# Preparing the second MoE's weights by pieces: one piece to three matmul groups instead of one to two attention slots

## The chip, the cores and the metric

The program runs on one core of one Trainium2 chip. The metric is device time in microseconds (us). In the core, TensorE (PE) multiplies matrices, VectorE (DVE), ScalarE (ACT) and GpSimd (POOL) work on tiles, and the queue of SyncE (SP) issues nearly all DMAs, in its order. Each engine carries out its own instructions in the order in which they stand in the program, and waits on semaphores for the others.

## The reference

Attention with a memory term, then two feed-forward blocks over 2304 tokens of 512 numbers (4 batches of 576):

```
scores = scale * q k^T, causal;  a = softmax(scores)         # B,H,S,D = 4,8,576,64
phi(x) = elu(x) + 1;  mem = (phi(q) M_prev) / (phi(q) z_prev)
x = g * mem + (1 - g) * (a v)                                # as [2304, 512]
h = x @ w_in;   x = (h * sigmoid(h)) @ w_out                 # first MoE,  d_ff 2048
g = x @ w_gate; v = x @ w_val
out = (g * sigmoid(g) * v) @ w_out2                          # second MoE, d_ff 1536
```

The weights come as float64, the rest as float32.

## The kernel before

**First half.** Attention and the first MoE run together. Attention is cut into units (a batch and a pair of heads), a unit into steps, and the steps of all units are laid out in numbered slots (`slots`, 177 of them, 0 to 176). Attention's tiles live in pools that are opened one after another, `atA`, `atB`, `atF` and `atG` (batches 2 and 3); `open_G` also starts the generator `prep_w2`. The first MoE is a generator too (`moe1`): 32 segments (a block of 256 or 320 tokens by a slice of four 128-columns of w_in), each with four groups of 12 matmuls into h (L785) and four groups of 12 into y (L843), 256 groups in all; each gives one item. After a group into h follow `th` on ACT (L792) and DVE (L793), `gh` on ACT (L194) and `gl` on POOL (L795), which the groups into y read. There are two `th` buffers and, while attention runs, three PSUM banks for h and y; later eight. The main loop takes item after item and runs attention slots as goals require.

**The second MoE's weights.** It multiplies float32 weights as a high and a low part, so the float64 weights are decoded and split first, in 12 columns j of three tiles each (w_gate, w_val, w_out). One step of `prep_w2` takes a piece: `next_tile` decodes one tile of 128x512 numbers (`t2`; ACT L660, DVE L661 to L663), and `halves` splits tiles on ACT (L194) and POOL (L908) into `wo` tiles, which SP stores to DRAM (L893). Four sums `S2` on POOL (L919 to L922) belong to each column. Five steps make a column, three of them with a decode: 36 decodes, called pieces below. While attention runs, every second slot takes a step. When it has ended, `open_w2` takes over, one turn at each item: it finishes the column in work, closes attention's pools, opens new ones, issues the first `y_prep` (the second MoE's input, 768 tokens of it, summed and split: DVE L968 to L979, ACT L961, POOL L962), then takes a prep step at every second item, and last loads the 12 `wo` tiles of the second MoE (L1006).

**The second MoE** (L1044, L1112) then runs on PE in an order written out by hand, with its weights streamed (`stream`, L1027) through the ring `wp` of eight buffers that the first MoE's weights (`w<-wd`, L689) use as well.

**What sets the order.** Outside that hand-written part the framework places the instructions: it goes by the order in which the Python code issues them, by what each waits for and by its own estimate of times, and may put an instruction of a later step ahead of one of an earlier step on its engine. So a prep step may stand in an engine's order at another place than where the loop issued it.

## Time and profile before

| | |
|---|---|
| median of 3 runs | 1149.1 us (1147.8 to 1150.14) |
| the profiled execution, its own time | 1152.71 us |
| its span, first to last instruction | 1150.9 us |
| mean granted clock of PE | 0.98 |
| busy: PE, DVE, POOL, ACT | 95%, 57%, 48%, 45% of the span |

The profile has a row for each group of instructions, with busy time, mean duration and what ended the idle time before it, and can be asked for stretches of the span. A name in a row is `out<-in` with buffer numbers left out; "L793" is a line of the kernel; the granted clock 1.00 is 2.4 GHz and 0.50 is 1.2 GHz. PE is the busiest engine, so what counts is where it waits and where its clock is lower. An idle DVE or POOL costs nothing by itself. The first MoE fills the time from about 40 to 720 us, attention ends near 595 us, and the second MoE follows to the end.

### The profile page before, as it was taken

The numbers are of one execution on the slowest core, as the hardware profiler recorded it, in microseconds if no ns is written. First come the engines' busy times: TensorE is split into PE (matmuls) and PEld (weight loads), VectorE is DVE, ScalarE is ACT, GpSimd is POOL, SyncE is SP. The second block draws the span as 40 slices with busy tenths as digits, with TensorE's granted clock in tenths as the row PEclk, the third lists the DMA queues.
The fourth block names the chain that finished last, engine by engine and source line by source line (L and its number), as shares of the span: only waits on it lengthen the run. The fifth ranks groups of instructions, "written<-read, shape, count | busy, mean of one in ns | idle before, by whom it ended". The sixth has DMA issues, their size and how long they took to land.

```text
span 1150.9 us, 19093 instructions
## 1 busy us (share of the span) xinstructions
PE 1095.0 (95%) x6803; PEld 981.6 (85%) x6803; DVE 652.1 (57%) x1413; ACT 516.7 (45%) x1237; POOL 557.2 (48%) x566
## 2 busy tenths in 40 slices
PE   7899999988989999999996899899999999999998
PEld 5577877887889889999895899799989999999986
DVE  6986777789897885336748653333363333333320
ACT  6754766456665665526534443122342323323222
POOL 4565575579897895315539875111171112312123
PEclk9989999998989999999999899999999999999999
DMA  8965755567788763442237989866674555555501
GB/s 215 297 204 184 239 174 169 168 210 244 235 295 319 242 208 107 144 139 85 78 107 250 339 291 348 317 192 192 192 249 154 177 171 166 182 165 182 165 28 55
DMA packets 155919, 226.72 MB, mean 197 GB/s; under 512 B 75696, under 2 KB 108464, under 8 KB 155824
## 3 DMA queue, kind: packets, MB, share of 16 engines
q1 hardware_dynamic: 153648, 225.10, 60.1%
q8 instruction: 54, 0.88, 0.3%
q10 hardware_dynamic: 2176, 0.40, 0.2%
q14 instruction: 41, 0.34, 0.1%
HBM read 170.93 MB, written 54.53 MB: 196 GB/s over the span
## 4 chain that ended last, share of the span: by engine, by line
PE 71%; DVE 11%; POOL 7%; DMA 3%; ACT 3%; issue 3%; SPq 0%; POOLq 0%; ACTq 0%; DVEq 0%
PE po L1112 13%; PE y L843 12%; PE h L785 12%; PE gb L1044 9%; PE ga L1044 6%; PE U L554 3%; PE gd L1044 3%; PE gc L1044 3%; PE pst L321 3%; PE pss L421 2%; POOL s L463 2%; DVE t L662 2%; POOL wo L908 2%; DVE t L661 1%; DMA w<-wg 1%
## 5 line engine op out<-in xcount | busy, mean ns | idle before, releaser
L1098 POOL TENSOR_TENSOR pl<-r,ph 128x384 fp32r<-128x384 f32 x72 | 74.4, 1042 | 320.7 <-ACT ph L1097 259.5
L785 PE MATMUL h<-xh,w 128*128 128x256 f32 (+1 forms) x1024 | 173.6, 308 | 23.8 <-DVE th L793 20.2
L843 PE MATMUL y<-gh,w 128*128 128x320 f32 (+1 forms) x1024 | 175.1, 306 | 3.0 <-DMA w<-wd 1.6
L785 PEld LDWEIGHTS h<-xh,w 128*128 128x128 f32 x1024 | 148.4, 194 | 33.1 <-DVE th L793 21.6
L795 POOL TENSOR_TENSOR gl<-th,gh 128x256 fp32r<-128x256 f32 (+1 forms) x128 | 115.1, 903 | 120.4 <-ACT gh L194 79.8
L843 PEld LDWEIGHTS y<-gh,w 128*128 128x128 f32 x1024 | 147.5, 192 | 16.3 <-issue 9.1
L463 POOL TENSOR_TENSOR s<-s,r 128x128 f32<-128x128 f32 (+4 forms) x144 | 123.8, 890 | 63.3 <-DVE r L480 30.3
L1112 PE MATMUL po<-wo,ph 128*128 128x512 f32 x432 | 134.2, 396 | 2.9 <-ACT ot L1118 1.8
L1044 PE MATMUL gb<-yT,w 128*128 128x384 f32 x648 | 132.4, 339 | 3.7 <-DMA w<-wg 2.3
L1044 PEld LDWEIGHTS gb<-yT,w 128*128 128x128 f32 x648 | 116.4, 188 | 13.8 <-issue 2.6
L1071 DVE TENSOR_TENSOR gd<-gb,e 128x384 f32<-128x384 f32 x36 | 20.4, 567 | 151.7 <-PE gb L1044 148.9
L793 DVE SCALAR_TENSOR_TENSOR th<-th,h 128x256 f32<-128x256 f32 (+1 forms) x128 | 56.8, 448 | 72.8 <-ACT th L792 72.7
L843 PE MATMUL y<-gl,w 128*128 128x320 f32 (+1 forms) x512 | 94.9, 300 | 2.1 <-POOL gl L795 2.1
L785 PE MATMUL h<-xl,w 128*128 128x320 f32 (+1 forms) x512 | 94.3, 304 | 0.0
L194 ACT CAST gh<-th 128x256 fp32r<-128x256 f32 (+1 forms) x128 | 54.7, 432 | 80.5 <-DVE th L793 46.5
L1112 PEld LDWEIGHTS po<-wo,ph 128*128 128x128 f32 x432 | 79.3, 188 | 11.8 <-ACT ot L1118 2.6
L1044 PE MATMUL ga<-yB,w 128*128 128x384 f32 x432 | 88.1, 339 | 0.0
L1112 PE MATMUL po<-wo,pl 128*128 128x512 f32 x216 | 84.5, 399 | 0.7 <-POOL pl L1098 0.7
L430 ACT ACTIVATE s<-s,mn 128x256 f32<-128x256 f32 (+3 forms) x128 | 71.3, 558 | 23.4 <-DVE mn L426 22.5
L843 PEld LDWEIGHTS y<-gl,w 128*128 128x128 f32 x512 | 77.3, 191 | 4.8 <-POOL gl L795 2.5
L785 PEld LDWEIGHTS h<-xl,w 128*128 128x128 f32 x512 | 78.2, 195 | 3.1 <-issue 2.6
L1044 PEld LDWEIGHTS ga<-yB,w 128*128 128x128 f32 x432 | 77.7, 190 | 2.1
(141 smaller groups left out, 2028.2 us busy)
## 6 DMA issues: line engine op xcount, KB each, us to landing
w<-wg SPq DMA_DIRECT2D x108, 512.0 KB, 4.2
w<-wd SPq DMA_DIRECT2D x80, 512.0 KB, 4.8
wg<-wo SPq DMA_DIRECT2D x36, 512.0 KB, 5.0
wd<-w SPq DMA_DIRECT2D x32, 512.0 KB, 4.0
raw<-in_moe_w_out_dram SPq DMA_DIRECT2D x28, 512.0 KB, 4.3
wo<-wo SPq DMA_DIRECT2D x24, 512.0 KB, 5.7
w<-wg SPq DMA_DIRECT2D x36, 256.0 KB, 3.4
raw<-in_moe_w_in_dram SPq DMA_DIRECT2D x16, 512.0 KB, 5.5
```

Of the source, the lines that this page charges most:

```text
L194: nc.scalar.copy(out, in_)
L321: nc.tensor.matmul(dst, src, ident[0:n, 0:n], start=start, stop=True, is_transpose=True, skip_group_check=True)
L430: nc.scalar.activation(out=a, in_=a, func=ACTF.Exp, scale=-1.0, bias=mn, accum_out=o["sm", sup][:, col:col + 1])
L463: nc.gpsimd.tensor_mul(a, a, r.to_broadcast([P, w]))
L554: nc.tensor.matmul(U[64 * hh:64 * hh + 64, c0:c1], row_of("v", c)[:, hh], a(hh), start=False, stop=(m == len(todo) - 1), skip_group_check= ...
L785: nc.tensor.matmul(ps[:, :nt], w[:, kk, :], x[:, kk, :nt], start=(m == 0), stop=(m == 3 * KD - 1))
L793: nc.vector.scalar_tensor_tensor(th[:, :nt], th[:, :nt], 1.0, ps[:, :nt], ALU.add, ALU.mult)
L795: tt(CFG["gl" if n >= CFG["n0"] else "gl0"]).tensor_sub(gl[:, :nt], th[:, :nt], f(gh[:, :nt]))
L843: nc.tensor.matmul(ps[:, :nt], w[:, c], g[:, :nt], start=(m == 0), stop=(m == last))
L1044: nc.tensor.matmul(dst, ws[nw][wi][:, P * kk:P * kk + P], y[ny][:, yi, kk], start=(start and m == 0), stop=(stop and m == 5), skip_group_c ...
L1098: nc.gpsimd.tensor_sub(pl, r, f(ph))
L1112: nc.tensor.matmul(po[t], a[:, c], w, start=(j == 0 and n == 0), stop=(j == F2 - 1 and n == 2))
```

## The change

A prep step is no longer tied to the attention slots (`attn_slot`) but to the items of the first MoE: while attention runs, every third item takes one. After attention the generator yields twice a step until the pools are switched, and afterwards three items go by for each step instead of two. From then on `next_tile` loads up to three raw tiles ahead (`raw8`) instead of two.

```diff
--- before.py
+++ after.py
@@ -50,6 +50,7 @@
     blks=1,
     pw=3,
     pt=4,
+    every=3,
     p_ring=15,
     pp=4,
     op=2,
@@ -633,8 +634,6 @@
     def attn_slot(s):
         for st in slots[s]:
             st()
-        if "prep" in ph2 and s % 2 == 0:
-            next(ph2["prep"], None)
 
 
     w1 = {}
@@ -898,7 +897,7 @@
             raw = raws.pop(0)
             t = decode(raw, cur["pw"].tile([P, 512], F32, tag="t", name="t2", bufs=CFG["pt"]))
             flush()
-            fetch(2)
+            fetch(ph2.get("ahead", 2))
             return t
 
         def halves(src, n, dst):
@@ -984,6 +983,7 @@
         ph2["hold"] = True
         for x in ph2["prep"]:
             yield
+            yield
             if x == "empty":
                 break
         cur["x"].close()
@@ -994,12 +994,14 @@
         del ph2["hold"]
         with ExitStack() as x:
             cur["raw"] = x.enter_context(tc.tile_pool(name="rawp2", bufs=CFG["raw"], side="right"))
+            ph2["ahead"] = CFG["raw8"]
             cur["pw"] = x.enter_context(tc.tile_pool(name="pw2", bufs=1, side="right"))
             y0 = y_prep(0)
             for _ in ph2["prep"]:
                 yield
                 next(y0, None)
-                yield
+                for _ in range(CFG["every"] - 1):
+                    yield
         ph2["wo"] = ctx.enter_context(tc.tile_pool(name="wo", bufs=1, side="right"))
         for j in range(F2):
             wos[j] = ph2["wo"].tile([P, 4, 256], F32, name=f"wo{j}")
@@ -1127,6 +1129,7 @@
         items = moe1()
         next(items)
         slot, n_g = 0, 0
+        every = CFG["every"]
         goals, cost, prevc = [], 0, 0
         for sg in segs:
             r = ready[sg["b"], sg["blk"][0] // SA]
@@ -1156,7 +1159,10 @@
                 elif slot < NSLOT:
                     attn_slot(slot)
                     slot += 1
-                if slot >= NSLOT:
+                if slot < NSLOT:
+                    if "prep" in ph2 and n_g % every == 0:
+                        next(ph2["prep"], None)
+                else:
                     if "late" not in ph2:
                         ph2["late"] = open_w2()
                     next(ph2["late"], None)
```

What that makes of the engines' orders is seen at three places. `t2` is a decoded piece, `th` the first MoE's h on its way to `gh`, `s` and `mn` belong to attention. First, DVE in the stretch of attention after the 60th `th`. Before, from one `th` to the next:

```order
L793 SCALAR_TENSOR_TENSOR th_5423<-th_5423,h_5410 128x320
L426 ISA s00_5450,mn0_5442<-pss_5444,mask_64 128x128
L426 ISA mn0_5442 128x1
L426 ISA s01_5462,mn0_5442<-pss_5456,mask_64 128x256
L426 ISA mn0_5442 128x1
L426 ISA s10_5453,mn0_5442<-pss_5445,mask_64 128x128
L426 ISA mn0_5442 128x1
L426 ISA s11_5465,mn0_5442<-pss_5457,mask_64 128x256
L426 ISA mn0_5442 128x1
L793 SCALAR_TENSOR_TENSOR th_5487<-th_5487,h_5474 128x320
```

and now, at the same `th` (th_5532 is what th_5487 was):

```order
L427 ISA s10_5504,mn0_5493<-pss_5496,mask_64 128x128
L427 ISA mn0_5493 128x1
L427 ISA s11_5516,mn0_5493<-pss_5508,mask_64 128x256
L427 ISA mn0_5493 128x1
L660 TENSOR_SCALAR t2_7733<-t2_7733 128x512
L661 SCALAR_TENSOR_TENSOR t2_7733<-raw8_7282,t2_7733 128x512
L427 ISA s02_5559,mn1_5551<-pss_5553,mask_64 128x384
L427 ISA mn1_5551 128x1
L662 SCALAR_TENSOR_TENSOR t2_7733<-raw8_7282,t2_7733 128x512
L427 ISA s12_5562,mn1_5551<-pss_5554,mask_64 128x384
L427 ISA mn1_5551 128x1
L792 SCALAR_TENSOR_TENSOR th_5532<-th_5532,h_5519 128x320
```

Two decodes stand there now. Counted over DVE's whole order, the pieces decoded ahead of the 48th `th` are 17 in both, between the 48th and the 60th they were 7 and are 9, between the 60th and the 72nd 0 and 4; the rest, 12 before and 6 now, stand behind attention's end, all behind the 98th `th`.

Second, DVE some 35 us after attention's end. `yt`, `ytop` and `ybot` belong to `y_prep`, here to its second call, which the framework has moved up to here. Before:

```order
L793 SCALAR_TENSOR_TENSOR th_8016<-th_8016,h_8003 128x320
L793 SCALAR_TENSOR_TENSOR th_8046<-th_8046,h_8033 128x320
L661 TENSOR_SCALAR t2_8211<-t2_8211 128x512
L662 SCALAR_TENSOR_TENSOR t2_8211<-raw8_8031,t2_8211 128x512
L793 SCALAR_TENSOR_TENSOR th_8068<-th_8068,h_8055 128x256
L663 SCALAR_TENSOR_TENSOR t2_8211<-raw8_8031,t2_8211 128x512
L968 TENSOR_TENSOR yt_9750<-ytop_9748 128x768
L793 SCALAR_TENSOR_TENSOR th_8097<-th_8097,h_8084 128x256
```

and now (th_8059, th_8088 and th_8110 are what th_8016, th_8046 and th_8068 were):

```order
L792 SCALAR_TENSOR_TENSOR th_8059<-th_8059,h_8046 128x320
L967 TENSOR_TENSOR yt_9750<-ytop_9748 128x768
L660 TENSOR_SCALAR t2_8579<-t2_8579 128x512
L974 TENSOR_TENSOR ytop_9748<-ybot_9749,ytop_9748 128x2x384
L792 SCALAR_TENSOR_TENSOR th_8088<-th_8088,h_8075 128x320
L661 SCALAR_TENSOR_TENSOR t2_8579<-raw8_8264,t2_8579 128x512
L792 SCALAR_TENSOR_TENSOR th_8110<-th_8110,h_8097 128x256
L662 SCALAR_TENSOR_TENSOR t2_8579<-raw8_8264,t2_8579 128x512
```

The subtraction into yt_9750, which needs the loaded ytop_9748, stood behind three `th` and stands behind one. On POOL the order from attention's end to the second `gl` behind the seven splits of `y_prep` is the same as before.

Third, SP at the end of the first half: the loads of the 12 `wo` tiles (`wo0` to `wo11`), the first MoE's weights (`wd1_20` to `wd1_23` are its last) and the second MoE's (`wg`). Before:

```order
L893 DMA wg11_3_8584<-wo_8636 128x512
L689 DMA w_8900<-wd1_23_2318 128x1024
L893 DMA wo11_8682<-wo_8683 128x1024
L1027 DMA w_9088<-wg0_0_3425 128x1024
L1027 DMA w_9090<-wg0_1_3426 128x1024
L852 DMA yd_69<-yp_7795 128x256
L1006 DMA wo0_8720<-wo0_3704 128x1024
L1006 DMA wo1_8736<-wo1_4384 128x1024
L1006 DMA wo2_8760<-wo2_4991 128x1024
```

and now:

```order
L1008 DMA wo8_8816<-wo8_7655 128x1024
L1008 DMA wo9_8838<-wo9_7917 128x1024
L1008 DMA wo10_8856<-wo10_8266 128x1024
L1008 DMA wo11_8874<-wo11_8586 128x1024
L688 DMA w_8523<-wd1_12_1011 128x1024
L688 DMA w_8545<-wd1_13_1108 128x1024
L688 DMA w_8561<-wd1_14_1178 128x1024
L688 DMA w_8577<-wd1_15_1260 128x1024
L688 DMA w_8678<-wd0_16_1729 128x1024
```

A row `wo11_8682<-wo_8683` is a store of a prepared tile to DRAM, `wo0_8720<-wo0_3704` a load from there. Lines are one lower in the changed kernel up to L1000 and two or more higher behind. The `wo` loads were behind all of the first MoE's weights and the first two `wg` loads; they now stand ahead of `wd1_12`, twelve loads earlier. In the same queue the load of `wd1_4` stood behind the store of the first column prepared after attention and now also waits behind the first two stores of the next column (`wg11_0`, `wg11_1`).

## Rows read from the trace of the kernel before

**Rows 1.** stretches of the span: stretch, its length, busy us of each engine, clock, DMA

```profile
250.00:292.00 42.00, 33.49 (x205) 30.30 (x204) 41.05 (x77) 24.10 (x61) 39.12 (x37) 0.88 0.76 240
292.00:355.00 63.00, 58.36 (x417) 53.86 (x416) 54.56 (x108) 39.61 (x104) 52.80 (x53) 0.95 0.78 257
355.00:417.00 62.00, 59.58 (x428) 54.77 (x427) 50.44 (x118) 36.70 (x92) 49.76 (x53) 1.00 0.84 285
417.00:472.00 55.00, 54.53 (x410) 50.23 (x409) 34.71 (x80) 32.69 (x83) 34.46 (x38) 1.00 0.38 119
600.00:660.00 60.00, 46.30 (x308) 44.54 (x307) 44.66 (x50) 26.83 (x57) 51.75 (x41) 0.89 0.84 301
660.00:720.00 60.00, 60.00 (x445) 60.00 (x444) 26.93 (x46) 23.44 (x53) 37.89 (x37) 1.00 0.87 316
720.00:740.00 20.00, 14.66 (x69) 12.65 (x69) 5.51 (x11) 3.20 (x7) 2.45 (x2) 0.93 0.94 356
```

**Rows 2.** line L793 alone on DVE, in stretches from the start: busy, count

```profile
0.00:355.00 355.00, 21.20 (x48) 0.96 0.71 219
0.00:417.00 417.00, 26.44 (x60) 0.97 0.73 229
0.00:472.00 472.00, 31.91 (x72) 0.97 0.69 216
```

**Rows 3.** tile t (a decoded piece) alone, in two stretches

```profile
417.00:472.00 55.00, 0.00 (x0) 1.03 (x2) 2.03 (x2) 1.00 0.38 119
595.00:705.00 110.00, 37.35 (x36) 14.31 (x24) 30.04 (x28) 0.94 0.82 293
```

**Rows 4.** one group of POOL instructions: line, names, count, busy, mean ns, idle

```profile
L908 POOL TENSOR_TENSOR wo<-S,wo 128x512 fp32r<-128x512 f32 x24 | 35.2, 1474 | 7.2 <-ACT wo L194 4.4 <-issue 1.2 <-PE pss L449 0.7
```

**Rows 5.** PE in order of time: start, length, line, shape, count, wait

```profile
331.74 2.50 PE L785 MATMUL h<-xh,w 128*128 128x320 f32 x8 [2.73 <-DVE th L793]
631.42 2.08 PE L785 MATMUL h<-xh,w 128*128 128x256 f32 x8 [7.26 <-DVE th L793]
643.54 1.33 PE L785 MATMUL h<-xh,w 128*128 128x320 f32 x8
646.54 0.59 PE L843 MATMUL y<-gh,w 128*128 128x256 f32 x3 [1.08 <-DMA w<-wd]
649.95 2.50 PE L785 MATMUL h<-xh,w 128*128 128x320 f32 x8 [1.62 <-DVE th L793]
727.72 1.29 PE L1044 MATMUL gb<-yT,w 128*128 128x384 f32 x6 [2.29 <-DMA w<-wg]
```

**Rows 6.** three stretches of five us, columns as in rows 1

```profile
330.00:335.00 5.00, 3.26 (x12) 3.26 (x13) 3.15 (x4) 3.22 (x7) 4.86 (x7) 0.61 1.04 330
335.00:340.00 5.00, 5.00 (x34) 4.96 (x33) 4.77 (x8) 3.43 (x9) 4.92 (x5) 0.71 0.93 318
650.00:655.00 5.00, 5.00 (x20) 5.00 (x21) 2.14 (x3) 1.42 (x4) 5.00 (x7) 0.50 1.04 408
```

**Rows 7.** line L662 on DVE: shortest, median and longest duration in ns

```profile
L662 DVE SCALAR_TENSOR_TENSOR t<-raw,t x36: 676/1107/1791, 241.1 to 678.0; 128x512 int32<-128x512 int32 x36
```

**Rows 8.** POOL in order of time around 627 us

```profile
626.87 2.24 POOL L962 TENSOR_TENSOR yT<-ytop,yT 128x768 fp32r<-128x768 f32 x1
629.08 1.30 POOL L795 TENSOR_TENSOR gl<-th,gh 128x320 fp32r<-128x320 f32 x1
```

**Rows 9.** DVE in order of time around 634 us

```profile
633.48 0.49 DVE L793 SCALAR_TENSOR_TENSOR th<-th,h 128x320 f32<-128x320 f32 x1 [2.11 <-ACT th L792]
638.36 1.57 DVE L968 TENSOR_TENSOR yt<-ytop 128x768 f32<-128x768 f32 x1
```

**Rows 10.** SP, which issues the DMAs, in order of time

```profile
630.75 0.39 SPq L952 DMA_DIRECT2D ytop<-yd  x1
641.53 1.78 SPq L689 DMA_DIRECT2D w<-wd  x3
706.22 8.97 SPq L1006 DMA_DIRECT2D wo<-wo  x12
```

## The prediction

> **What bounds the kernel now.** I read the stretches of the span first, and look in each row at PE's busy time, its granted clock, and how full DVE and POOL are [rows 1]. PE is the bound nearly everywhere: between 660 and 720 us it is busy for 60.00 of 60 us. It loses time at three places that the change touches. From 250 to 417 us, with attention, first MoE and decoding together, it is idle for 8.5, 4.6 and 2.4 us of the three stretches, and the granted clock is 0.88, 0.95 and 1.00. From 600 to 660 us, just behind attention, it is idle for 13.7 of 60 us at a clock of 0.89. From 720 to 740 us, where the second MoE starts, it is idle for 5.3 of 20 us at 0.93.
>
> The next view is PE in order of time, with the waits in brackets [rows 5]. The longest are a wait of 2.73 us at 331.7, one of 7.26 us at 631.4 and one of 1.62 us at 650.0, all for a `th` of DVE; one of 1.08 us at 646.5 for a load of w; and one of 2.29 us at 727.7 for a load of the second MoE's weights. Behind a wait the clock is lower, at 1.2 GHz in the worst case: at 650.0 eight matmuls of 128x320 take 2.50 us, at 643.5 the same eight take 1.33. So one stall in attention costs more than its wait: 2.73 us idle, and then a clock of 0.61 for the 3.26 us that PE works in the next five and of 0.71 for five more [rows 6], 1.3 + 1.4 = 2.7 us. I call that an event of 5.4 us.
>
> **What moves, and what a piece costs.** Nothing is added or removed in arithmetic. Of 36 decoded pieces, 12 stood behind attention's end and 6 will. The trace has the 48th, 60th and 72nd `th` done by 355, 417 and 472 us [rows 2], so by the counts in the order two of the six moved pieces fall between 355 and 417 and four between 417 and 472 us; in the second stretch DVE decodes nothing today [rows 3]. The twelve late pieces take 37.35 us of DVE and 30.04 us of POOL without the split sums, 3.1 and 2.5 each [rows 3]; the split sums add 35.2 us over all 36, 1.0 each [rows 4]. A moved piece is thus 3.1 us of DVE and 3.5 of POOL, beside its raw load and its stores, which go from a stretch with the DMA engines busy 0.84 to 0.87 to stretches with 0.84 and 0.38 [rows 1].
>
> *Attention, 355 to 472 us.* DVE goes from 50.4 to 56.6 us of 62 (91%) and POOL from 49.8 to 56.8 (92%); in the second stretch DVE from 34.7 to 47.1 of 55 (86%) and POOL from 34.5 to 48.5 (88%). Both have room, so at the lower end the pieces are free, and as the framework reshuffles attention around them, the waits of today could also shrink: I put the lower end at -4 us, about half of what these stretches and the one before lose in idle time. The nearest row for such filling is 292 to 355, with DVE at 87% and POOL at 84%: 4.6 us idle and 5% of the clock, 3.2 us, 7.8 in all. If both stretches became like it, that would be 5.3 us more in the first (7.7 less 2.4) and 6.3 in the second, the upper end of 11.6. But what that row loses is mostly one event, the 5.4 us above, so I count in events: none, one or two. I take one, +5.4 us. It would show where a decode stands ahead of a `th`, as in the first place of the order.
>
> Here a rule of the Trainium skill speaks against the change. The row: the second decoding step, with two SBUF inputs, takes from 676 to 1791 ns for one shape, median 1107 [rows 7]. The page SBUF — State Buffer, section Who interferes with whom, says that VectorE with two SBUF inputs and a GpSimd instruction that reads SBUF exclude each other, the second to start waiting for the first. The trace agrees that something stretches this step; if in the fuller stretches each of the two such steps of a moved piece took the longest duration instead of the median, four pieces would bring 4 x 2 x 0.68 = 5.5 us more of DVE to the second stretch, 96% of it, and by that rule two events are likelier than one, 5.4 us more.
>
> *Behind attention, 595 to 660 us.* I expect the big wait to stay. At 631.4 PE waits for a `th` whose buffer a `gl` on POOL has to free, and that `gl` starts at 629.1 behind splits of `y_prep`, the last of which takes 2.24 us [rows 8]. The order of POOL and of DVE up to there is the same in the changed kernel, and so is what they wait for, raw tiles that can only be loaded when attention's pools close. So 13.7 us of idle time mostly remain. Behind it two things change. DVE's subtraction into yt_9750 now stands ahead of the second `th`, which ran at 633.5, while that subtraction ran at 638.4 when ytop had landed, 7.6 us after its issue at 630.8 [rows 9, 10]. With no raw load ahead in the queue it can be issued when the split at 626.9 has ended (629.1), and with fewer loads in flight it may land in 4 to 7.6 us, at 633 to 637; then come 1.6 us and two more steps of some 2 us together, so that `th` is 3 to 7 us late. And the load of `wd1_4`, issued at 641.5 [rows 10], now waits for the splits up to `wg11_1`, four more POOL instructions of a piece and a `gl` or two, some 5 us. PE has other groups into h to do meanwhile (eight banks), and the order gives it three ahead of that y. Against it go the waits of 1.08 and 1.62 us and the five us at clock 0.50 [rows 5, 6], 2.5 us lost, which have another shape then. Below, all of those 5.2 us are gained; above, 4 us are lost. I take +1. Between 660 and 720 us the other six pieces leave DVE and POOL, but PE is busy throughout there, so that is worth nothing.
>
> *Start of the second MoE, 720 to 740 us.* Today SP issues the 12 loads into `wo` over 9.0 us from 706.2 [rows 10], ahead of the `wg` loads, and PE waits 2.29 us for one of these. Those 12 go ahead of `wd1_12` now, some 45 us earlier, so this wait goes. At most the whole loss of the stretch goes, 5.3 us idle plus 7% of 20 us in clock, 6.7. What is late next is ACT and DVE of the first products, which nothing changes. I take -3.5: the 2.29 and about the clock behind it. At their new place the `wo` loads could delay `wd1_12` to `wd1_15`; four groups into h stand ahead of the y that needs them, so I count nothing, and up to 3 us if that cover is short.
>
> **Sum.** 5.4 + 1 - 3.5 = +2.9 us: the profiled execution of 1152.71 us (span 1150.9 and 1.8 around it) would become 1155.6. It is 3.6 us above the median of the runs; on that median the sum gives 1152.0 us. With the ends left as they are worked out, -4 to +11.6, -5.2 to +4 and -6.7 to 0.
>
> **Rivals.** *Faster.* The pieces cost attention nothing, since POOL and DVE are only 63% busy from 417 to 472 us, and the second half of the stall behind attention goes with the lighter DMA queue: -5.2, and at the start -2.3 and 2 of the 2.4 other idle and clock: -4.3. Together -9.5, 1139.6 us. For it speaks that the trace has PE at full clock with 15 or more us of room on both engines exactly where the pieces go; against it, that the order behind attention brings a `th` and a load later. It needs `ytop` to land by 633 us. *Slower.* DVE is what bounds attention once it is above 90%: two events, 10.8, with 3 behind attention and -2.3 at the start, +11.5, 1160.6 us. It decides from the point where two strings of decodes and attention steps stand ahead of a `th` for longer than PE has groups to do; the stretch 250 to 292, with DVE at 98% and PE idle for 8.5 of 42 us, is its picture [rows 1]. The rule above is on its side. *The pacing does little.* The framework has already moved pieces wherever there was room, and the six more find it without an event: 0 + 1 - 3.5, -2.5, 1146.6 us.
>
> **How the numbers follow.** My forecast has 0.40, faster 0.27, slower 0.16, little effect 0.17. A measurement of this kernel can tell about 0.2%, 2.3 us, from no change. Of the forecast, 3 us either way from 1152.0, I give 0.26 to slower, 0.12 to the same and 0.02 to faster; the faster and the slower rival count whole; of the last, whose middle lies at the bound, 0.09 is faster and 0.08 the same. That is faster 0.38, same 0.20, slower 0.42. Cases of both signs have most of the chance: the forecast's own range is 1149 to 1156, and the range for 8 in 10 goes to the middle of the faster rival and of the slower one, 1140 to 1161.
>
> **What would show it.** The forecast is right if, in the stretches up to the 72nd `th`, PE has one more wait of 2 to 4 us for DVE with a low clock behind it; if PE still waits about 7 us in the 40 us behind attention's end, for POOL by way of `th`; and if the wait for `wg` at the second MoE's start is gone. It is wrong if PE's idle time up to the 72nd `th` is as before or less (then the faster rival or the last), if the wait behind attention is shorter than 5 us, or if PE comes to wait for `wd1_12`.

## The result and the profile after

The changed kernel takes 1163.07 us (median of 4 runs, 1162.39 to 1164.36) against 1148.79 us (1147.8 to 1150.14) for the kernel before on the same chip: a ratio of 1.0125 with an interval of 1.0107 to 1.0142, or some 14 us slower. The profiled execution took 1163.68 us, its span is 1161.9 against 1150.9 us. The two traces thus hold 11.0 of the 14 us; the other 3 are there because the profiled execution of before, at 1152.71, was slower than its timed runs.

The stretches of the changed kernel, with the columns of [rows 1]: stretch, length, busy us and count of PE, its weight loads, DVE, ACT and POOL, granted clock, DMA share, GB/s.

```profile
250.00:292.00 42.00, 33.24 (x214) 30.13 (x212) 41.43 (x78) 25.18 (x63) 39.12 (x36) 0.92 0.77 245
292.00:355.00 63.00, 56.55 (x400) 51.55 (x400) 55.76 (x108) 38.94 (x101) 53.47 (x54) 0.95 0.81 250
355.00:417.00 62.00, 56.79 (x389) 52.70 (x388) 48.57 (x103) 35.98 (x87) 49.68 (x52) 0.92 0.84 285
417.00:472.00 55.00, 50.20 (x358) 44.86 (x357) 44.79 (x99) 31.98 (x81) 46.52 (x49) 1.00 0.65 225
472.00:540.00 68.00, 66.17 (x475) 62.55 (x474) 27.34 (x75) 31.43 (x80) 27.36 (x34) 0.97 0.47 144
600.00:660.00 60.00, 49.90 (x331) 47.49 (x330) 39.52 (x45) 25.81 (x54) 44.28 (x35) 0.86 0.56 200
660.00:720.00 60.00, 57.87 (x430) 57.43 (x430) 15.83 (x35) 17.96 (x46) 19.70 (x24) 1.00 0.85 319
720.00:740.00 20.00, 20.00 (x139) 19.80 (x139) 8.95 (x14) 5.47 (x11) 9.27 (x6) 1.00 0.36 114
```

The reader is to see three things. From 355 to 540 us PE works less than before; the granted clock is 0.92 from 355 to 417 and 0.97 from 472 to 540 us, where it was 1.00, and 1.00 as before from 417 to 472. DVE and POOL are no fuller than before from 355 to 417 (48.57 and 49.68 us against 50.44 and 49.76). And from 660 to 720 us POOL is down from 37.89 to 19.70 us, which gains nothing. For before, 472 to 540 us was not shown yet:

```profile
472.00:540.00 68.00, 67.65 (x502) 64.00 (x501) 31.04 (x87) 30.87 (x83) 25.88 (x30) 1.00 0.42 136
```

I put idle time and clock into one number, the time that PE loses in a stretch: its length less the busy time, plus the busy time by (1 - clock). This table has it for all kernels below, in us:

```
stretch from        250   292   355   417   472   540   600   660   720   740
before             12.5   7.6   2.4   0.5   0.3   0.0  18.8   0.0   6.4   0.6
after              11.4   9.3   9.8   4.8   3.8   0.0  17.1   2.1   0.0   2.1
e1 attention only  12.5   8.2   8.7   5.4   3.8   0.0  14.3  13.3   0.6   1.5
e2 late only       12.5   7.2   2.4   0.5   0.3   0.0  15.7   2.4   4.6   0.0
e4 slots 5 of 8    12.5   7.3   2.3  10.7   2.8   0.0  14.9   4.8   1.6   0.5
e5 40 steps        11.4   9.3   9.8   4.3   0.0   0.4  15.5   2.1   0.8   1.0
e6 wo late         12.5   8.2   8.8   5.5   3.8   0.0  16.2   1.0   0.2  12.6
e7 POOL only       12.5   7.1   2.5  11.6   2.0   0.0  15.5   3.3   3.4   2.0
e8 DVE only        12.5   7.6   2.8   8.7   0.4   0.0  16.5   2.0   2.6   1.9
g1 all held         6.7   8.9   2.0  15.3   6.5   0.6   1.6   2.0   1.4   0.0
g3 last 12 held    12.0  10.4   2.3   0.6   5.9   2.4   1.9   2.0   1.4   0.0
g6 held, gap        6.5   5.9   2.5   9.2   3.0   4.5   5.9   2.0   0.6   0.0
g7 held, wide gap   7.8   7.8   2.0   5.3  11.9   1.4   4.9   3.6   0.6   0.0
g9 one in 3, held   5.5   9.6   2.8   8.3   3.7   0.7  12.7   9.8   2.3   1.2
```

(Each stretch ends where the next begins, the last at 800 us.) The number has limits: a PE that is busy at full clock counts as no loss, and the clock is read to a hundredth. Over the whole span, span less loss is 1067 to 1076 us by kernel, so a few us between two kernels' sums say little. Before and after lie close in this (1076 and 1075 us). Between 250 and 600 us the changed kernel loses 39.1 us and the kernel before 23.3: 15.8 more. Between 600 and 800 us it loses 21.3 and the kernel before 25.8: 4.5 less. Together that is the 11 us of the spans.

PE of the changed kernel in order of time (start, length, line, shape, count, wait in brackets) at its longest waits behind 300 us:

```profile
327.53 0.44 PE L417 MATMUL pss<-Kh,S 128*128 128x128 f32 x1 [4.11 <-DVE tb L197]
382.18 0.45 PE L417 MATMUL pss<-Kh,S 128*128 128x128 f32 x1 [3.17 <-ACT tb L195]
384.12 0.77 PE L417 MATMUL pss<-Kh,S 128*128 128x128 f32 x2 [1.49 <-DVE tb L197]
645.90 2.08 PE L784 MATMUL h<-xh,w 128*128 128x256 f32 x8 [5.67 <-DVE th L792]
652.36 2.07 PE L784 MATMUL h<-xh,w 128*128 128x256 f32 x8 [2.46 <-DVE th L792]
696.73 1.18 PE L842 MATMUL y<-gh,w 128*128 128x256 f32 x8 [2.13 <-DMA w<-wd]
```

The first three are of a kind that [rows 5] does not have: PE waits there not for the first MoE but for attention's own `tb`, the softmax tiles, transposed and copied to SBUF. These copies free PSUM buffers of one pool (`ps_a`), and the next scores (`pss`) take their buffers from the same pool. The wait at 327.53 stands where before waited 2.73 us for a `th`, at 331.7; the first scores of the unit at 382 and 384 waited for `tb` before as well, but 0.68, 0.15 and 0.24 us, at 391.3 to 392.7. Read back from 382: PE has transposed the tiles (`pst`) by 379.0, but ACT copies them into `tb` only behind the next unit's splits (`S`, `Kh`). These stand in its order behind the first step of a decode (L659), which waits for POOL's split of an earlier piece (L907). That split stands behind POOL's scaling of softmax tiles (L464), and the scaling waits for reciprocals on DVE, just ahead of which DVE works on two pieces:

```profile
363.07 1.30 DVE L661 SCALAR_TENSOR_TENSOR t<-raw,t 128x512 int32<-128x512 int32 x1
367.51 0.68 DVE L662 SCALAR_TENSOR_TENSOR t<-raw,t 128x512 int32<-128x512 int32 x1
368.64 0.15 DVE L481 TENSOR_TENSOR r<-r,omg 128x1 f32<-128x1 f32 x1
```

```profile
368.80 4.72 POOL L464 TENSOR_TENSOR s<-s,r 128x384 f32<-128x384 f32 x5 [4.97 <-DVE r L481]
373.48 1.29 POOL L907 TENSOR_TENSOR wo<-t,wo 128x512 fp32r<-128x512 f32 x1
```

```profile
374.80 0.68 ACT L659 ACTIVATE t<-raw 128x512 f32<-128x512 f32 x1 [1.65 <-POOL wo L907]
377.30 2.54 ACT L195 CAST Kh<-K 64x512 fp32r<-64x512 f32 x4
380.99 1.08 ACT L195 COPY tb<-pst 128x512 f32<-128x512 f32 x2
```

```profile
377.26 1.75 PE L322 MATMUL pst<-ident,s 128*128 128x128 f32 x14
```

ACT has no idle time between 374.80 and the end of these copies. PE carries out its order as it stands, so it waits. The two waits together take 4.66 us, and behind them the clock is 0.63, 0.50 and 0.84 in the steps of 5 us from 380 to 395. Of the 7.4 us that the stretch loses more, some 2.8 are idle time and the rest is the clock. From 417 to 540 us no wait shown is over 1.5 us; the longest are 1.41 us for `xl` at 433.7, 1.23 for a `th` at 458.3 and 0.89 for a `tb` at 479.4. At 645.90 stands the wait that was 7.26 us in [rows 5], now 5.67, and a second one of 2.46 behind it. The wait for `wg` at the second MoE's start [rows 5] is gone; in its place PE waits 2.13 us at 696.73 for a `wd` load that stands behind the 12 `wo` loads in SP's order.

### The profile page after: what moved, and what is told of

It reads as the page before. It is cut to its first block, busy times and chain, and to the rows that moved or that the text cites. A ratio compares the mean times of both kernels' runs of the same rounds, so it can differ in the third digit from the quotient of the medians.

```text
span 1161.9 us, 19100 instructions
## 1 busy us (share of the span) xinstructions
PE 1100.5 (95%) x6803; PEld 985.9 (85%) x6803; DVE 653.2 (56%) x1413; ACT 518.1 (45%) x1237; POOL 554.6 (48%) x566
## 4 chain that ended last, share of the span: by engine, by line
PE 69%; DVE 13%; DMA 5%; POOL 5%; issue 4%; ACT 4%; SPq 0%; ACTq 0%; POOLq 0%; DVEq 0%
PE y L842 13%; PE po L1114 12%; PE h L784 11%; PE gb L1046 9%; PE ga L1046 6%; PE U L555 3%; PE gd L1046 3%; PE gc L1046 3%; PE pst L322 2%; PE pss L422 2%; DMA wo<-wo 2%; POOL s L464 2%; DVE t L661 2%; PE pss L417 1%; DVE t L662 1%
## 5 line engine op out<-in xcount | busy, mean ns | idle before, releaser
L784 PE MATMUL h<-xh,w 128*128 128x320 f32 (+1 forms) x1024 | 170.7, 306 | 19.6 <-DVE th L792 15.8
L842 PE MATMUL y<-gh,w 128*128 128x320 f32 (+1 forms) x1024 | 181.5, 314 | 6.7 <-DVE th L792 4.2
L842 PEld LDWEIGHTS y<-gh,w 128*128 128x128 f32 x1024 | 152.9, 199 | 20.3 <-issue 9.3
L464 POOL TENSOR_TENSOR s<-s,r 128x128 f32<-128x128 f32 (+4 forms) x144 | 118.7, 854 | 64.6 <-DVE r L481 27.1
L842 PE MATMUL y<-gl,w 128*128 128x320 f32 (+1 forms) x512 | 97.7, 306 | 2.5 <-POOL gl L794 2.5
L1114 PEld LDWEIGHTS po<-wo,ph 128*128 128x128 f32 x432 | 79.1, 188 | 12.3 <-ACT ot L1120 3.1
L431 ACT ACTIVATE s<-s,mn 128x128 f32<-128x128 f32 (+3 forms) x128 | 71.3, 558 | 29.9 <-DVE mn L427 29.1
L842 PEld LDWEIGHTS y<-gl,w 128*128 128x128 f32 x512 | 79.8, 197 | 5.6 <-POOL gl L794 3.2
L791 ACT ACTIVATE th<-h 128x256 f32<-128x256 f32 (+1 forms) x128 | 51.6, 407 | 65.0 <-PE h L784 43.5
```

Source lines behind the costliest of these rows:

```text
L431: nc.scalar.activation(out=a, in_=a, func=ACTF.Exp, scale=-1.0, bias=mn, accum_out=o["sm", sup][:, col:col + 1])
L464: nc.gpsimd.tensor_mul(a, a, r.to_broadcast([P, w]))
L784: nc.tensor.matmul(ps[:, :nt], w[:, kk, :], x[:, kk, :nt], start=(m == 0), stop=(m == 3 * KD - 1))
L791: nc.scalar.activation(out=th[:, :nt], in_=ps[:, :nt], func=ACTF.Tanh, scale=0.5 / WS)
L842: nc.tensor.matmul(ps[:, :nt], w[:, c], g[:, :nt], start=(m == 0), stop=(m == last))
L1114: nc.tensor.matmul(po[t], a[:, c], w, start=(j == 0 and n == 0), stop=(j == F2 - 1 and n == 2))
```

## The experiments

All ratios are to runs of the kernel before on the same chip as the run itself. Their times are device us, medians of the runs.

**Which part of the change.** One kernel has only the new pacing while attention runs, one only the part behind attention:

```diff
 # e1: the kernel before, with
-        if "prep" in ph2 and s % 2 == 0:
-            next(ph2["prep"], None)
...
-                if slot >= NSLOT:
+                if slot < NSLOT:
+                    if "prep" in ph2 and n_g % 3 == 0:
+                        next(ph2["prep"], None)
+                else:
 # e2: the changed kernel, with the above taken back
```

> Only the pacing while attention runs is changed (a step at every third item instead of every second slot); the steps behind attention are paced and loaded as before the change. All theories put the loss in attention, so attention's end moves from 595 to about 611 us as in the changed kernel, and the time is 1163 us, 3 us either way. If it came in under 1155, the loss would belong to the late part of the change.

> Only the part behind attention is changed (two yields a step until the pools are switched, three items a step later, three raw tiles ahead); attention is paced by slots as before, so 24 pieces are decoded in it and 12 behind. Expected: attention ends at 595 us, and as 12 pieces are left the wo loads stay behind wd1_23 in SP's order, so nothing is gained at the second MoE's start either: 1149 us, 2 us either way. If the late part by itself lost, it would be above 1152.

Measured: e1 1168.2 us, ratio 1.0183 (1.0161 to 1.0206); e2 1148.6 us, 0.9998 (0.9986 to 1.0010). In the table e1 loses 38.7 us between 250 and 600 us, e2 23.0, as after and before. So the whole loss belongs to the pacing in attention, and the late part by itself does nothing. Beside the new pacing it is worth some 6 us (1.0183 against 1.0125), by where the `wo` loads come to stand. e1 came out 2 us above its range: SP issues ten of the `wo` loads there between two loads into `w`, at 676.48 and 685.25 us, and PE waits longer for such a load than the changed kernel does at 696.73:

```profile
695.92 1.41 PE L841 MATMUL y<-gh,w 128*128 128x256 f32 x5 [7.39 <-DMA w<-wd]
```

**The second MoE's start.** The changed kernel with the `wo` loads held back to the first MoE's last segment. They then stand behind all of its weights again, one load further back than before the change:

```diff
 # e6
         wos[j] = ph2["wo"].tile([P, 4, 256], F32, name=f"wo{j}")
-        nc.sync.dma_start(out=wos[j], in_=wdo[j])
-        yield
...
             gs[n][j] = (gh, gl)
+            if n + 1 == len(segs) and ji == 2:
+                for jj in range(F2):
+                    nc.gpsimd.tensor_copy(r_(wos[jj][:, 0, 0:1]), th[:, 0:1])
+                    nc.sync.dma_start(out=wos[jj], in_=wdo[jj])
```

> The changed kernel, but the 12 loads into wo wait (by a one-column copy on POOL into each wo tile) for a th of the first MoE's last segment, and so stand behind wg0_2 in SP's order, where they stood behind wg0_1 before the change. If the early wo loads are what shortened the second MoE's start by some 5 us, the wait for wg comes back: 1165 to 1169 us, less up to 2 us for the wait for wd1_12 that the early loads cause. If the start gained for another reason, 1161 to 1164 us.

Measured: 1169.79 us, 0.8 above the range, ratio 1.0183 (1.0164 to 1.0202), 6.7 us above the changed kernel. The wait is back, longer than the 2.29 us of [rows 5]:

```profile
746.66 1.62 PE L1048 MATMUL gb<-yT,w 128*128 128x384 f32 x4 [6.03 <-DMA w<-wg]
```

So the early `wo` loads are what the start gained. The 6.7 us are more than the table's gain of 4.9, and the wait is longer than before; whether the one place further back makes that difference was not tested.

**Number of pieces, or their order.** Two kernels part them: e4 has as many pieces in attention as the changed kernel, but by slots; e5 has the new order up to the 60th `th`, and three pieces fewer behind it.

```diff
 # e4: the kernel before, with
-        if "prep" in ph2 and s % 2 == 0:
+        if "prep" in ph2 and s % 8 in (0, 2, 3, 5, 6):
 # e5: the changed kernel, with
-                    if "prep" in ph2 and n_g % every == 0:
+                    if "prep" in ph2 and n_g % every == 0 and ph2.setdefault("n", 0) < 40:
+                        ph2["n"] += 1
```

> Paced by slots as before the change, but five slots of eight take a step instead of four, the rest as before: 30 pieces in attention as in the changed kernel, with the order up to the 58th th as before and the six more pieces between the 60th and the 72nd th. Theory one, the work of the six pieces on DVE and POOL is what costs: attention loses the same 16 us, its end near 611, about 1160 to 1163 us. Theory two, the order that the new pacing makes ahead of the 60th th is the larger half: the 7 us lost between 355 and 417 us and what is lost before are not lost here, only some 8 us of 417 to 540 us, and the gain of about 5 us at the second MoE's start stays: 1150 to 1154 us.

> The changed kernel, but the steps stop after 40 while attention runs: by the order the pieces up to the 60th th stand as in the changed kernel (9 between the 48th and the 60th), then one instead of four up to the 72nd, and nine are left behind attention. The changed kernel lost 9.8 us between 355 and 417 us (2.4 before the change) and 8.6 between 417 and 540 (0.8 before). If the two losses belong to the pieces of their own stretch, the first stays, 9 to 10, and the second falls to 1 to 4: 1154 to 1160 us. If what the new order loses later is carried on from the first stretch, the second stays at 7 to 9: 1161 to 1164 us.

Measured: e4 1160.52 us, ratio 1.0114 (1.0096 to 1.0132), in the range of its first theory; e5 1155.73 us, 1.0061 (1.0043 to 1.0080), in that of losses that belong to the pieces of their own stretch. First e4, then e5:

```profile
355.00:417.00 62.00, 59.72 (x434) 55.13 (x432) 50.54 (x120) 37.31 (x93) 47.99 (x52) 1.00 0.87 290
417.00:472.00 55.00, 45.21 (x321) 39.61 (x317) 47.15 (x87) 34.74 (x84) 52.01 (x50) 0.98 0.66 222
```

```profile
355.00:417.00 62.00, 56.79 (x388) 52.72 (x387) 48.57 (x103) 35.95 (x87) 49.69 (x52) 0.92 0.85 285
417.00:472.00 55.00, 52.30 (x374) 48.25 (x373) 38.88 (x96) 31.61 (x80) 39.43 (x45) 0.97 0.53 177
472.00:540.00 68.00, 68.00 (x507) 64.14 (x506) 30.40 (x74) 31.70 (x80) 24.77 (x30) 1.00 0.43 132
```

In e5 the stretch 355 to 417 us is that of the changed kernel to a hundredth in PE's and DVE's busy time, and loses the same 9.8 us, 7.4 more than before; it also has the waits at 382 and 384 (3.17 and 1.50 us). From 417 to 540 us it loses 4.3 instead of 8.6. So some 4 us belong to the three pieces it leaves out, and the first loss stands by itself. In e4, whose order is that of before up to the 58th `th`, the first stretch loses 2.3 us; the six pieces in the second cost 10 there and 2.5 behind it. So it is the number that costs in e4. In the changed kernel about half is lost from 355 to 417 us, where more pieces came together with a new order: two more by the order, one more by the time at which DVE ran them. Which of these it was at 382 us isn't parted; that DVE and POOL are no busier there speaks for the order. In e4 ACT is the link again. The longest wait of the second stretch, 2.44 us for a `tb` at 468.9, has ACT ahead of it waiting for stores of prepared tiles to free their buffers, with the next unit's `Q` behind, for which DVE stood idle for 4.61 us:

```profile
461.82 0.41 ACT L194 CAST wo<-t 128x256 fp32r<-128x256 f32 x1 [1.64 <-DMA wg<-wo]
463.53 0.62 ACT L194 CAST wo<-t 128x512 fp32r<-128x512 f32 x1 [1.30 <-DMA wg<-wo]
```

**DVE or POOL.** The kernel before, with idle work at e4's place: the POOL part of six pieces (e7) or the DVE part (e8), into scratch tiles, and the real pieces where they were.

```diff
 # e7: slots as in e4, raw loads of the columns from 8 on only after this; then
 # (in e8 the three decoding steps on DVE, from S, at part 0, 1 and 4)
+            if j == 8:
+                for n in range(10):
+                    part = n % 5
+                    if part >= 2:
+                        wx = cur["pw"].tile([P, 4, 256], F32, tag="o", name="wx", bufs=CFG["pw"])
+                        if part == 2:
+                            for _ in range(4):
+                                nc.gpsimd.tensor_sub(wx[:, 0], S[:, 0], S[:, 1])
...
+                        nc.gpsimd.tensor_sub(wx[:, 1:4:2], S[:, 0:2], S[:, 2:4])
+                    yield ("empty" if n == 9 and "hold" in ph2 else None)
```

> The kernel before with idle work added where the run with five slots of eight has its six more pieces (between the 60th and the 72nd th): only the POOL part of six pieces, eight splits of 128x512 and ten operations of 128x256 on POOL into a scratch tile, some 20 us of POOL, no DVE, ACT or DMA. All 12 last pieces stay behind attention, so the late part and the second MoE's start are as before. That run lost 12 us by the 72nd th. If POOL's queue is what holds attention up (the scaling of s and the gl stand behind the splits), this loses 8 to 12 us: 1157 to 1161. If DVE is what holds it up, under 3 us: 1149 to 1152. If both are needed, about half: 1153 to 1156.

> The same with only the DVE part of six pieces: 18 operations of 128x512 on DVE from and into SBUF at that place, 18 or so us of DVE, no POOL, ACT or DMA. If DVE holds attention up, 8 to 12 us: 1157 to 1161. If POOL does, under 3 us: 1149 to 1152. If both are needed, about half: 1153 to 1156.

Measured: e7 1161.43 us, ratio 1.0102 (1.0085 to 1.0118); e8 1159.57 us, 1.0078 (1.0061 to 1.0095). First e7, then e8:

```profile
417.00:472.00 55.00, 47.21 (x324) 42.07 (x325) 38.74 (x77) 27.78 (x71) 48.04 (x52) 0.92 0.32 102
```

```profile
417.00:472.00 55.00, 49.30 (x348) 44.95 (x348) 45.04 (x95) 30.11 (x76) 35.21 (x36) 0.94 0.35 110
```

Each run gave the answer of its own engine, so together they fit none of the three theories: either part alone loses most of what both lose together (12.4 and 8.7 us from 250 to 600, against 12.3 in e4). POOL is 87% busy in the one, DVE 82% in the other, and the other engine is at 70 and 64%. I read this as one chain that passes through both engines: lengthening it in either place holds PE up, and a second lengthening beside it adds little. That reading was not tested further. Two things limit it. About 5 us of e7 go with one DVE instruction that is told of at the end, so its 12.4 are not POOL's work alone. And neither kernel has the pieces' work on ACT or their stores. Such work stands ahead of `tb` in e4 and, at 374.80 us, in the changed kernel; what it costs by itself was not tested.

**Other places for the pieces.** Since the framework may move a piece ahead of its step, a step's place in the loop doesn't fix its time. Here the raw load itself is held back, by a one-column copy into the raw tile from the `gl` of the group just issued:

```diff
 # g1, g3: the changed kernel, with n_g % 2, and
+        if gate is not None:
+            nc.gpsimd.tensor_copy(raw[:, 0, 0:1].bitcast(F32), f(gate[:, 0:1]))
         w2 = w.bitcast(I32)
...
-                raws.append(load64((w2_gate, w2_val, w2_out)[part], j, part // 2))
+                raws.append(load64((w2_gate, w2_val, w2_out)[part], j, part // 2, ph2.get("gl")))
 # in g3 ph2.get("gl") only if 8 <= j
```

> The changed kernel with a step at every second item, and the raw loads of the last 12 pieces (columns 8 to 11) held back by a one-column copy on POOL from the gl of the group just issued, so that the framework cannot move them ahead: by the order two pieces stand between the 60th and the 72nd th, eight between the 72nd and 84th, two after; none is left behind attention. If what costs is a stretch that is too full, attention loses little, as DVE and POOL are busy only 31 and 26 of 68 us from 472 to 540: 0 to 4 us there, 5 us gained at the second MoE's start, 1 to 3 behind attention: 1141 to 1148 us. If any piece put into attention costs it 2 to 2.7 us, as the six did, 12 cost 24 to 32: 1165 us or more.

> As the run before, but all pieces' loads held back, so that the pieces spread evenly from the 32nd to the 88th th: 4, 8, 7, 7, 7 and 3 pieces in the stretches up to the 36th, 48th, 60th, 72nd, 84th and 98th th, where the kernel before has 8, 9, 7, 0, 0 and 0, and 12 behind attention. If fullness costs, the stretch 250 to 292, which loses 8.5 us idle, gains 2 to 6 us, the 7 pieces from the 60th to the 72nd cost 4 to 12: 1140 to 1152 us. If any piece costs about the same wherever it is put in attention, 1165 us or more.

Measured: g3 1144.72 us, ratio 0.9955 (0.9940 to 0.9970); g1 1145.28 us, 0.9958 (0.9943 to 0.9973). Both beat the kernel before and the changed one. First two stretches of g3, then two of g1:

```profile
472.00:540.00 68.00, 62.77 (x451) 58.34 (x450) 48.15 (x99) 39.45 (x96) 53.69 (x61) 0.99 0.84 287
600.00:660.00 60.00, 58.10 (x439) 56.38 (x438) 22.75 (x35) 24.05 (x54) 29.44 (x25) 1.00 0.72 270
```

```profile
250.00:292.00 42.00, 36.76 (x257) 35.19 (x255) 37.08 (x78) 29.32 (x70) 32.22 (x38) 0.96 0.70 228
417.00:472.00 55.00, 43.63 (x305) 40.44 (x305) 38.73 (x84) 27.79 (x70) 43.29 (x49) 0.91 0.55 185
```

The times lie in the range, but the way there was not the one I gave. Attention is not cheap: in all, g3 loses 33.6 us from 250 to 600 us and g1 40.1, where before loses 23.3. From 472 to 540 us g3 loses 5.9 us with DVE at 71% and POOL at 79%; g1 gains 5.8 us at 250 and loses 15.3 at 417, behind a wait of 5.01 us for `tb`, with DVE at 70% and POOL at 79%. What pays is the stretch behind attention, where the loss goes from 18.8 to 1.9 and 1.6 us: no piece is left there, POOL is busy for 29.44 us instead of 51.75 [rows 1], and PE's longest wait in it is gone though `y_prep`'s splits are still to be done; they now run when the `gl` ahead of them are through (g3):

```profile
631.27 1.34 POOL L796 TENSOR_TENSOR gl<-th,gh 128x320 fp32r<-128x320 f32 x1 [0.72 <-ACT gh L195]
632.57 1.86 POOL L964 TENSOR_TENSOR yB<-ytop,yB 128x768 fp32r<-128x768 f32 x1
634.39 2.57 POOL L964 TENSOR_TENSOR yT<-yt,yT 128x768 fp32r<-128x768 f32 x1
```

**Around the place that costs.** The last three hold all loads back and differ in pace:

```diff
-                    if "prep" in ph2 and n_g % every == 0:
+                    if "prep" in ph2 and n_g % 2 == 0 and not 116 <= n_g < 136:   # g6
+                    if "prep" in ph2 and n_g % 2 == 0 and not 112 <= n_g < 140:   # g7
+                    if "prep" in ph2 and n_g % 3 == 0:                            # g9
```

> The run with all pieces held back, but no step between the items 116 and 136, so that only two pieces stand between the 60th and the 72nd th (there were seven), 15 between the 72nd and the 98th, none behind attention. That run lost 5.8 us less than the kernel before in 250 to 292, 14.8 more in 417 to 472 and 6.2 more in 472 to 540, and 15 less behind attention. If it is the stretch with two units' steps close together that cannot take the pieces (417 to 472), its loss goes to under 2 us here and the later pieces cost 0 to 5 between 540 and 600: 1131 to 1138 us. If the pieces cost the same where they go to, 1143 to 1147 us.

> The same with no step between the items 112 and 140: no piece between the 60th and the 72nd th, 14 between the 72nd and the 98th, and three behind attention. By the first theory attention is as in the run before it or a little better, and the three late pieces with their raw loads cost 1 to 6 us of the 15 saved behind attention, if the loss there comes from pieces beside y_prep: 1133 to 1143 us. If the loss behind attention was due to y_prep's own splits alone, there is no difference to the run before it beyond 2 us.

> The changed kernel itself (a step at every third item) with all raw loads held back to where the loop issues them, so that the pace is kept: 4, 5, 4, 6, 4 and 5 pieces in the stretches up to the 36th, 48th, 60th, 72nd, 84th and 98th th, eight behind attention. Expected if 417 to 472 is the place that costs: 250 to 292 gains 5 us, 292 to 417 loses no more than before the change, six pieces in 417 to 472 cost 10, the eight late ones bring back some 15 us behind attention: 1146 to 1154 us. If the changed kernel's loss comes from the framework moving pieces ahead of their pace (bursts) rather than from their number in 417 to 472, that stretch costs under 4 us here: 1138 to 1145 us.

Measured: g6 1144.8 us, ratio 0.9964 (0.9951 to 0.9977); g7 1145.28, 0.9961 (0.9946 to 0.9976); g9 1150.67, 1.0011 (0.9998 to 1.0023). First two stretches of g6, then two of g7:

```profile
417.00:472.00 55.00, 50.32 (x359) 47.63 (x360) 32.43 (x80) 26.50 (x67) 31.32 (x38) 0.91 0.38 127
540.00:600.00 60.00, 55.47 (x398) 48.34 (x397) 49.91 (x123) 37.70 (x99) 48.72 (x55) 1.00 0.54 194
```

```profile
417.00:472.00 55.00, 49.68 (x352) 46.55 (x353) 38.41 (x85) 28.29 (x71) 32.74 (x40) 0.94 0.46 150
600.00:660.00 60.00, 51.99 (x366) 51.01 (x363) 34.84 (x45) 25.77 (x56) 45.12 (x43) 0.91 0.78 275
```

The gap did not take the loss away: g6 came in the range for pieces that cost the same wherever they go. g6 loses 9.2 us from 417 to 472 with two pieces in it and 4.5 from 540 to 600, g7 5.3 with none and 11.9 from 472 to 540. The pieces cost wherever they go, and the four held kernels without eight late pieces end within 0.6 us of each other. g7's three late pieces cost nothing that can be seen (8.5 against 7.9 us from 600 to 720, and 0.5 us of time). g9 is the changed kernel with nothing but the loads held back: 13 us faster than it by the two ratios, level with the kernel before. Its profiled execution, 1154.13 us, was the slowest of 12; its span is 9.6 us shorter than the changed kernel's, and the table has 3.8 of that. Against the changed kernel it gains 5.9 us at 250 to 292 and 7.0 at 355 to 417. From 417 to 472 it loses 8.3, so bursts alone are not what costs there. With eight pieces left behind attention it keeps most of the loss there: 12.7 us, with a wait of 5.10 us for `th` at 644.88.

## Why the prediction was wrong

*Sign.* I gave slower the largest chance (0.42), and slower it was; the size was missed. 1163.07 us lies 2 us above the range's end of 1161, and 11 above the 1152.0 of the sum. Of the rivals, the slower one came closest.

*Attention, the term that failed.* The step was "I take one, +5.4 us", resting on "Both have room". Measured: +15.8 us from 250 to 600 us, made of -1.1, +1.7, +7.4, +4.3 and +3.5 in its first five stretches. My upper end of 11.6 us was met in 355 to 472 us (11.7 more) but not for its reason. It stopped at 472, while the loss goes on up to 540, it had 5.3 and 6.3 in the two stretches where 7.4 and 4.3 were lost, and it took full stretches for it. They never became full. From 355 to 417 DVE was busy 78% and POOL 80%, where I had forecast 91 and 92; from 417 to 472, 81 and 85%, forecast 86 and 88. Busy share was thus the wrong measure of room: by the traces, what counted was what stood ahead of `tb` in the orders of ACT, POOL and DVE. The mark that I gave came, longer waits in these stretches and a lower clock behind them. But at the longest PE waits for `tb` inside attention, not for a `th` with a decode ahead of it. A slip beside it: the "15 or more us of room on both engines" that spoke for the faster rival hold for 417 to 472; from 355 to 417 there were 11.6 and 12.2 us.

*The slower rival* had nearly the right time for a wrong reason. It decided from "DVE above 90%", which was not reached. e7 and e8 show that 82 and 87% on one engine, with the other under 71%, do the same.

*The shared access of DVE and POOL*, for which I worked out 5.5 us by a rule of the Trainium skill (page SBUF — State Buffer, section Who interferes with whom), is at most a small part of the loss, as far as the decoding steps show. Over 355 to 540 us the decoding steps with two SBUF inputs became 0.15 and 0.14 us longer each, the one with one input 0.22 shorter (line, shapes, count, busy, mean ns; first before, then after):

```profile
L661 DVE TENSOR_SCALAR t<-t 128x512 int32<-128x512 int32 x7 | 6.4, 915 | 7.2 <-ACT t L660 7.2
L662 DVE SCALAR_TENSOR_TENSOR t<-raw,t 128x512 int32<-128x512 int32 x7 | 6.4, 914 | 0.1
L663 DVE SCALAR_TENSOR_TENSOR t<-raw,t 128x512 int32<-128x512 int32 x7 | 7.0, 1000 | 0.0
```

```profile
L660 DVE TENSOR_SCALAR t<-t 128x512 int32<-128x512 int32 x13 | 9.0, 694 | 4.7 <-ACT t L659 4.7
L661 DVE SCALAR_TENSOR_TENSOR t<-raw,t 128x512 int32<-128x512 int32 x13 | 13.8, 1063 | 0.2
L662 DVE SCALAR_TENSOR_TENSOR t<-raw,t 128x512 int32<-128x512 int32 x13 | 14.8, 1140 | 0.1
```

For the four pieces of my sum the two longer steps make 4 x 0.29 = 1.2 us instead of 5.5; with the third step, all 13 decodes took 13 x 0.07 = 0.9 us more.

*Behind attention.* I took +1, measured are +0.4 us from 600 to 720 (stretches of the span, in which attention now ends some 16 us later). The big wait stayed, 5.67 us, and the second `th` came late as forecast (2.46 us of wait where before had 1.62). PE did come to wait for the loads of `wd1_12` to `wd1_15`, 2.13 us, which I had priced at "up to 3 us if that cover is short", counted at nothing, and named among the signs of being wrong. That the six pieces which leave 660 to 720 us would gain nothing there was right.

*The second MoE's start.* I took -3.5, measured are -4.9 us from 720 to 800; e6 shows that the early loads make it.

*What I did not see.* That the loss behind attention, which I took as fixed by `y_prep`, depends on the pieces that run beside it. From 600 to 660 us the kernels with 12 late pieces lose 15.5 to 18.8 us (before, e2, e7, e8), those with six 14.3 to 17.1 (after, e1, e4, e6), g9 with eight 12.7, g7 with three 4.9, g1 and g3 with none 1.6 and 1.9. Half of the way there gains next to nothing, and this is why a change that moves half of the late pieces had no gain but that of the second MoE's start. The pieces are not all of it: g6 has none either and loses 5.9. Its `y_prep` splits begin on POOL 7 us behind attention's end, those of g1 and g3 some 22 us behind it. How much of the gain is due to their later start was not parted.

## What to carry to other kernels

Room in an engine's busy share is no room in a chain that passes through it. With DVE and POOL some 80% busy, the six pieces put beside attention cost 2.6 us each (15.8 in all); with the loads held back, 12 cost 0.7 to 1.4 each by the table (g6, g3, g1). The price is to be read from which matmuls wait and what stands ahead of their operands' makers. Where a scheduler orders the program, a step's place in a loop sets no pace; a data dependence on the load does, and here it was worth 13 us for the same pacing (g9). And a wait behind a burst may go only when the last of the burst goes, so look whether a move empties the place or halves it.

## What the runs showed of the hardware

A DVE instruction with two small SBUF inputs was held up once for as long as POOL worked without a gap. In e7 one multiplication of 128x4, whose line takes 0.15 to 1.23 us in the kernel before, took 8.16 us; POOL had ten instructions back to back, and DVE's ended when the last of them did, at 451.4 us:

```profile
443.23 8.16 DVE L391 TENSOR_TENSOR n<-n,g_bc 128x4 f32<-128x4 f32 x1
451.31 0.15 DVE L389 TENSOR_SCALAR n<-psm 128x6 f32<-128x6 f32 x1
```

```profile
442.27 1.29 POOL L924 TENSOR_TENSOR wx<-S 128x512 f32<-128x512 f32 x1
443.50 0.75 POOL L795 TENSOR_TENSOR gl<-th,gh 128x256 fp32r<-128x256 f32 x1
444.18 0.76 POOL L920 TENSOR_TENSOR wx<-S 128x256 f32<-128x256 f32 x1
...
449.39 1.30 POOL L924 TENSOR_TENSOR wx<-S 128x512 f32<-128x512 f32 x1
450.61 0.76 POOL L920 TENSOR_TENSOR wx<-S 128x256 f32<-128x256 f32 x1
```

The matmuls on `psk` waited 4.95 us and began at 451.95, just behind DVE's next steps. The trace names no releaser for this wait; that it comes from the multiplication is read from the times. The Trainium skill's page SBUF — State Buffer, section Who interferes with whom, says that such a DVE instruction and a GpSimd one that reads SBUF exclude each other. By that rule the trace agrees in kind; that the wait outlasted nine further instructions of POOL, not one, is what this run shows. It is no rule: in the kernel before POOL is busy for 20.00 of 20 us from 610 to 630 us, and the longest decoding step with two SBUF inputs that begins there takes 2.34 us.
